# Rank counts on two engines, narrower rows and unread products in the selection of a gated recurrence with a capacity-limited mixture of experts

## The chip, the cores and the metric

The kernel runs on one core of a Trainium2 chip. A core has five engines with queues of their own: TensorE (PE, matmuls; PEld is its weight load), VectorE (DVE), ScalarE (ACT), GpSimd (POOL) and SyncE (SP, which here issues the large transfers), beside 16 DMA engines. The metric is the device time of one execution in microseconds, 254.26 as the median of three runs before the change (253.77 to 255.12).

## The reference, cut to what matters

```python
sig = 1.0 / (1.0 + np.exp(-f_logit))                 # x, f_logit: (4, 5056, 256)
f = lower_bound + (1.0 - lower_bound) * sig
for t in range(S):
    h = f[:, t] * h + (1.0 - f[:, t]) * x[:, t];  y[:, t] = h
X = y.reshape(20224, 256);  logits = X @ w_gate      # 8 experts
expert_idx = argmax(logits);  gate_w = softmax(logits)[expert_idx]
for e in range(8):                                   # the 80 tokens of highest gate_w among e's
    tok = top_80(gate_w[expert_idx == e])
    out[tok] = gate_w[tok, None] * (np.maximum(X[tok] @ w1[e], 0.0) @ w2[e])   # F = 1024
# every other row of out is zero
```

## The kernel before, in words

Stage 1 (to about 145 us). Forty units of 512 tokens of one sequence (the last group 448) are loaded, turned to channels on PE (`sp`, `up`, L226), scanned on DVE (L243), kept in SBUF as `h_all`, and multiplied with the gate weights (`lg`, L255). For each group of four units the logits are turned (`lt`, L270), the largest is taken and the softmax value of the chosen expert is turned back (`ct`, L343) into `cand`: 128 rows, one for each expert and each position modulo 16, with 1280 candidates each. SP's queue carries loads, and among them writes of zeros that clear the output (L149).

Stage 2, the selection. Each row's 16 highest values are found (`vals`, L496 to 499). The rows of an expert must agree on its 80 highest: `spread` and a matmul with `mates` put the 16 x 16 values of an expert's rows side by side in PSUM (`rivals`, 256 columns, L506). For each of a row's 16 values one DVE instruction counts how many rivals are greater (`beat`, `rank`, L524). `taken` marks ranks under 80; two matmuls sum the counts (`sums_p`, L533, L534); `put` makes one-hot slots (L544), and 16 matmuls place token numbers and values in `flat_p` (L547). From it come `trow` (token numbers as integers, L549), the slots turned to partitions (`slots_down`, L479 to 486) and `doubts`, flags for a slow branch that does the selection in full if a row has more than 16 candidates of use. `max_index` (L511) and POOL (L467 to 518) find the token numbers meanwhile.

Stage 3, the experts. `gather` copies the 80 columns of an expert from `h_all`, with three engines side by side: DVE 28, ACT 28, POOL 24 columns. `scaled` (DVE), `hidden` (first layer, `h_ps`, L612), `relu` (ACT, L620), `result` (second layer, `y_ps`, L627), `finish` (DVE) and `scatter` (POOL) follow. Each engine works its queue in the order in which the code records it: the order is written out by hand. Weights arrive in halves of 512 KB in a ring of 7 buffers, in the order of a list (`order`); three entries (6 halves) are issued before the last clears, the rest as buffers come free (`more`), each issue standing in SP's queue.

Of the kernel before, what the change touches and what calls it, by code (L numbers as in the profile page):

```python
# [23 lines left out]
def kernel(  # L24
# [23 lines left out]
    DEEP = 2 * TOP  # L48
# [82 lines left out]

    hpool = tc.alloc_tile_pool(name="hpool", bufs=1, side="right")
# [23 lines left out]
    def clear_rest():  # L156
        clear_some(len(zeros) % R)
        for k, _ in zeros[::R]:
            clear(k)
        zeros.clear()  # L160

    with tc.tile_pool(name="ld", bufs=4) as ld, \
# [119 lines left out]
        def shifted(g):  # L282
            by_token(g)
            n_p = run(g)
            lg, _ = lts[g]
            full = [n_p, C, E]
            if g == begin(g):
                shs[g] = gsm.tile([P, per_batch, C, E], F32, name="shift", tag="shift")
                ohs[g] = gsm.tile([P, per_batch, C, E], BF16, name="oh", tag="oh", bufs=2)
                if any(run(k) < P for k in range(*batch_of(g))):  # L290
                    nc.gpsimd.memset(shs[g], 0.0)
            mx = gsm.tile([P, C], F32, name="mx", tag="mx")[:n_p]
            nc.vector.tensor_reduce(mx, lg, AX.X, ALU.max)  # L293
            nc.vector.tensor_tensor(lg, lg, mx.unsqueeze(2).broadcast_to(full), ALU.subtract)  # L294
            nc.scalar.copy(shs[begin(g)][:n_p, g - begin(g)], lg)  # L295
# [138 lines left out]
    order = [(1, 0)]  # L434
    for e in range(E):
        order += ([(1, e + 1)] if e + 1 < E else []) + [(2, e)]
# [54 lines left out]
    with tc.tile_pool(name="sel", bufs=1) as sel, \  # L491
         tc.tile_pool(name="psl", bufs=1, space=PSUM) as psl:
        vals = sel.tile([P, DEEP], F32, name="vals")
        rest = sel.tile([P, NP * TOP], F32, name="rest")
        flat_tops = tops.rearrange("p n t -> p (n t)")
        nc.vector.max(out=vals[:, :TOP], in_=flat_tops)  # L496
        nc.vector.match_replace(out=rest, in_to_replace=vals[:, :TOP], in_values=flat_tops,
                                imm_value=-2.0)
        nc.vector.max(out=vals[:, TOP:], in_=rest)
# [5 lines left out]
        rivals = psl.tile([P, C * DEEP], F32, name="rivals", tag="rivals")  # L505
# [3 lines left out]
        at = sel.tile([P, DEEP], U32, name="at")  # L509
        for k in range(0, DEEP, TOP):  # L510
            nc.vector.max_index(out=at[:, ds(k, TOP)], in_max=vals[:, ds(k, TOP)],  # L511
                                in_values=cand)
        ids = sel.tile([P, DEEP], F32, name="ids")
# [7 lines left out]
        rank = sel.tile([P, DEEP], F32, name="rank")  # L521
        beat = sel.tile([P, C * DEEP], F32, name="beat")
# [3 lines left out]
        taken = sel.tile([P, DEEP], F32, name="taken")  # L526
        some = sel.tile([P, DEEP], F32, name="some")
        count = sel.tile([P, 1], F32, name="count")
        nc.vector.tensor_scalar(some, vals, 0.0, None, ALU.is_gt)
        nc.vector.scalar_tensor_tensor(out=taken, in0=rank, scalar=float(capacity), in1=some,  # L530
                                       op0=ALU.is_lt, op1=ALU.mult, accum_out=count)
        sums_p = psl.tile([P, 2], F32, name="sums_p", tag="sums_p")
        nc.tensor.matmul(sums_p[:, 0:1], before, count, start=True, stop=True)  # L533
        nc.tensor.matmul(sums_p[:, 1:2], mates, count, start=True, stop=True)  # L534
# [3 lines left out]
        off = sel.tile([P, 2], F32, name="off")  # L538
# [6 lines left out]
        flat_p = psl.tile([2 * E, K], F32, name="flat_p", tag="flat_p")  # L545
        for j in range(DEEP):
            nc.tensor.matmul(flat_p, what[:, DEEP - 1 - j].rearrange("p i e -> p (i e)"),  # L547
                             put[:, j], start=j == 0, stop=j == DEEP - 1)
        nc.vector.tensor_copy(trow, flat_p[:E])  # L549
        flat = consts.tile([2 * E, K], F32, name="flat")  # L550
        nc.vector.tensor_copy(flat, flat_p)

        low = sel.tile([P, DEEP], F32, name="low")
        d = doubts
        nc.gpsimd.tensor_scalar(out=low, in0=taken, scalar1=-2.0, scalar2=2.0,
                                op0=ALU.mult, op1=ALU.add)
        nc.gpsimd.tensor_tensor(low, low, vals, ALU.add)
# [7 lines left out]
        nc.vector.tensor_scalar(d[:, 3:4], off[:, 1:2], float(capacity), None, ALU.is_gt)  # L567
        slots_down(flat, psl)
# [6 lines left out]
    def experts(again):  # L575
        with tc.tile_pool(name="xp", bufs=2) as xp, \
             tc.tile_pool(name="mp", bufs=2) as mp, \
             tc.tile_pool(name="psd", bufs=1, space=PSUM) as psd, \
# [77 lines left out]
            for e in range(E):  # L656
# [11 lines left out]
                if e > 0:  # L668
                    scatter(e - 1)
# [92 lines left out]
```

## Time and profile before

| | |
|---|---|
| runs, us | 254.26, 255.12, 253.77 |
| the profiled execution | 254.13 us, of which its span is 252.2 |
| busy: PE, DVE, ACT, POOL | 198.6 (79%), 171.5 (68%), 134.3 (53%), 135.5 (54%) us |
| mean granted clock of TensorE | 0.899 |
| moved by DMA | 81.09 MB, mean 321 GB/s |

Busy time is an average over three stages with different limits, so the share of an engine says little here. The profile's slices show where the stages lie, the chain of waits shows which work ended last, and the timeline shows single instructions with the idle time of their engine before them. A matmul of f32 operands shows as two instructions.

### The profile page before, as it was taken

How to read it: one execution, taken by the hardware profiler on the slowest of the kernel's cores; microseconds unless marked ns; L12 is line 12 of the kernel's file. 1: busy time of each engine (PE TensorE's matmuls, PEld its weight loads, DVE VectorE, ACT ScalarE, POOL GpSimd, SP SyncE). 2: the span in 40 equal slices, each digit the busy share in tenths (PEclk: the TensorE clock that was granted, in tenths of full speed). 3: DMA queues.
4: the chain of work that ended last, by engine and by line, in shares of the span. 5: the costliest groups of instructions: out<-in, count | busy, mean ns of one | idle time of the engine just before them, and what ended most of it. 6: DMA issues, size and time to landing. Idle time of an engine off the chain costs nothing.

```text
span 252.2 us, 5978 instructions
## 1 busy us (share of the span) xinstructions
PE 198.6 (79%) x1755; PEld 155.6 (62%) x1755; DVE 171.5 (68%) x484; ACT 134.3 (53%) x390; POOL 135.5 (54%) x275
## 2 busy tenths in 40 slices
PE   0679999999998799999699832016199999999990
PEld 0567676767675577667466521016199788888860
DVE  0898879696967697898689677982655066656200
ACT  1678868686879677767958510000625545455100
POOL 2758769595865969675669110300764066661111
PEclk9999999999999999999999965557555899999997
DMA  6999999999999999999999999999954599999700
GB/s 176 382 386 384 384 382 394 390 390 391 395 386 391 392 390 392 393 391 389 318 313 360 304 380 408 347 321 318 295 184 148 187 276 312 318 305 306 241 18 21
DMA packets 59384, 81.09 MB, mean 321 GB/s; under 512 B 3280, under 2 KB 52048, under 8 KB 56912
## 3 DMA queue, kind: packets, MB, share of 16 engines
q1 hardware_dynamic: 57888, 78.92, 90.9%
q10 hardware_dynamic: 1072, 1.06, 1.2%
q0 software_dynamic: 384, 0.66, 0.8%
q8 instruction: 16, 0.26, 0.4%
q14 instruction: 24, 0.20, 0.3%
HBM read 78.91 MB, written 22.41 MB: 402 GB/s over the span
## 4 chain that ended last, share of the span: by engine, by line
PE 56%; DMA 10%; DVE 9%; issue 8%; ACT 7%; POOL 4%; SPq 3%; POOLq 0%; DVEq 0%; ACTq 0%
PE h_ps L612 14%; PE y_ps L627 11%; PE lg L255 10%; PE sp L226 9%; PE up L226 7%; DMA x_t<-in_x_dram 4%; POOL x_t L219 4%; ACT h_all L237 4%; DVE beat L524 3%; DMA out_dram<-z_dram 3%; DMA f_t<-in_f_logit_dram 3%; DVE h_all L243 2%; PE flat_p L547 2%; PE lt L270 2%; ACT ls L262 1%
## 5 line engine op out<-in xcount | busy, mean ns | idle before, releaser
L219 POOL TENSOR_TENSOR x_t<-f_t,x_t 128x1024 f32<-128x1024 f32 (+1 forms) x40 | 94.8, 2377 | 39.3 <-ACT f_t L215 22.0
L243 DVE TENSOR_TENSOR_SCAN h_all<-h_all,up 128x512 f32<-128x512 f32 (+1 forms) x80 | 95.2, 1240 | 5.2 <-ACT h_all L237 4.3
L237 ACT ACTIVATE h_all<-sp,nomlb 128x512 f32<-128x512 f32 (+1 forms) x80 | 50.1, 677 | 15.3 <-PE sp L226 15.1
L226 PE MATMUL sp<-ident,f_t 128*128 128x128 f32 (+1 forms) x320 | 45.0, 285 | 10.4 <-ACT f_t L215 8.2
L226 PEld LDWEIGHTS sp<-ident,f_t 128*128 128x128 f32 (+1 forms) x320 | 35.5, 145 | 26.9 <-issue 21.1
L255 PE MATMUL lg<-h_all,wg 128*32 128x128 f32 (+1 forms) x640 | 43.5, 401 | 5.2 <-ACT ls L262 3.7
L226 PE MATMUL up<-ident,x_t 128*128 128x128 f32 (+1 forms) x320 | 43.1, 277 | 4.7 <-POOL x_t L219 2.7
L215 ACT ACTIVATE f_t<-f_t 128x1024 f32<-128x1024 f32 (+1 forms) x40 | 42.6, 1064 | 6.9 <-DMA f_t<-in_f_logit_dram 6.7
L612 PE MATMUL h_ps<-xt,w_sb 128*128 128x80 f32 x256 | 36.4, 311 | 7.0 <-issue 7.0
L594 ACT COPY xe<-h_all 128x2 f32 x224 | 22.2, 191 | 36.5 <-issue 30.4
L612 PEld LDWEIGHTS h_ps<-xt,w_sb 128*128 128x128 f32 x256 | 36.1, 227 | 7.8 <-issue 7.3
L226 PEld LDWEIGHTS up<-ident,x_t 128*128 128x128 f32 (+1 forms) x320 | 36.2, 143 | 7.0 <-POOL x_t L219 4.1
L594 DVE COPY xe<-h_all 128x2 f32 x224 | 26.6, 180 | 14.7 <-issue 14.7
L594 POOL COPY xe<-h_all 128x2 f32 x192 | 24.2, 193 | 15.0 <-DVE goal L486 8.2
L627 PE MATMUL y_ps<-w_sb,hid 128*80 128x256 f32 x128 | 29.6, 387 | 0.0
L255 PEld LDWEIGHTS lg<-h_all,wg 128*32 128x32 f32 x640 | 18.1, 118 | 18.2 <-ACT ls L262 5.9
L636 POOL DMA_INDIRECT out_dram<-y,goal x8 | 7.5, 939 | 32.4 <-DVE y L633 30.0
L627 PEld LDWEIGHTS y_ps<-w_sb,hid 128*80 128x80 f32 x128 | 19.2, 154 | 7.9 <-issue 0.7
L620 ACT ACTIVATE hid<-h_ps 128x320 f32<-128x320 f32 x16 | 7.0, 436 | 22.5 <-PE h_ps L612 18.1
L633 DVE TENSOR_SCALAR y<-y_ps,gsl 80x256 f32<-80x256 f32 x8 | 3.8, 480 | 19.9 <-PE y_ps L627 19.9
L295 ACT COPY shift<-lt 128x128 f32<-128x128 f32 (+1 forms) x10 | 2.6, 265 | 16.6 <-DVE lt L294 16.6
L293 DVE TENSOR_REDUCE mx<-lt 128x16 f32<-128x128 f32 (+1 forms) x10 | 2.9, 291 | 12.5 <-PE lt L270 12.3
(103 smaller groups left out, 104.8 us busy)
## 6 DMA issues: line engine op xcount, KB each, us to landing
f_t<-in_f_logit_dram SPq DMA_DIRECT2D x36, 512.0 KB, 7.0
x_t<-in_x_dram SPq DMA_DIRECT2D x36, 512.0 KB, 7.4
w_sb<-in_moe_w_dram SPq DMA_DIRECT2D x32, 512.0 KB, 4.7
out_dram<-z_dram SPq DMA_DIRECT2D x40, 256.0 KB, 7.3
out_dram<-z_dram SPq DMA_DIRECT2D x9, 1024.0 KB, 17.4
f_t<-in_f_logit_dram SPq DMA_DIRECT2D x4, 448.0 KB, 7.5
x_t<-in_x_dram SPq DMA_DIRECT2D x4, 448.0 KB, 7.7
z_dram<-zero ACTq DMA_DIRECT2D x1, 1024.0 KB
```

Of the source, the lines that this page charges most:

```text
L215: nc.scalar.activation(s_t, s_t, ACT.Sigmoid, scale=-1.0)
L219: nc.gpsimd.tensor_tensor(u_t, sts[n], u_t, ALU.mult)
L226: nc.tensor.transpose(ps[:, ds(r * k, k)], src[n][:, r, ds(o * P, P)], ident[:k, :k])
L237: nc.scalar.activation(columns(n, o), sps.pop((n, o)), ACT.Identity, scale=nomlb[:, ds(o, 1)], bias=1.0)
L243: nc.vector.tensor_tensor_scan(h, h, ups.pop((n, o)), h_all[:, o, ds(spot(n) - 1, 1)] if n >= B else 0.0, ALU.mult, ALU.add)
L255: nc.tensor.matmul(lgs[g][ds(r * LC, LC), b, :k], wg[:, o], columns(n, o)[:, r::R], start=o == 0, stop=o == DC - 1, skip_group_check=True)
L524: nc.vector.tensor_scalar(beat, rivals, vals[:, ds(k, 1)], 0.0, ALU.is_gt, ALU.add, accum_out=rank[:, ds(k, 1)])
L594: copy(X[e][:, :, ds(k + j, 1)], h_all[:, :, ds(v, 1)])
L612: nc.tensor.matmul(h_ps[:, c], halves[i][:, o, ds(c * P, P)], xt[:, o], start=o == 0, stop=o == DC - 1, skip_group_check=True)
L620: nc.scalar.activation(HID[e][:, ds(i * CH, CH)], ps[i], ACT.Relu)
L627: nc.tensor.matmul(y_ps, hid[:, c], halves[c // CH][:, c % CH], start=c == 0, stop=c == FC - 1)
L636: nc.gpsimd.indirect_dma_start(out=out, out_offset=bass.IndirectOffsetOnAxis(ap=goal[:, ds(e, 1)], axis=0), in_=Y.pop(e), in_offset=None, ...
```

## The change

- **Depth.** A row keeps 12 values instead of 16 (`DEEP`), so `rivals` has 192 columns, `put` 960 and the placing 12 matmuls.
- **Ranks on two engines.** DVE counts for 5 of them (`BY_DVE`); ACT takes the other 7, each as a sum of signs over `rivals`, recorded ahead of DVE's. Two small instructions join the two.
- **Unread products.** `busy` records plain products of the identity on PE, whose results nobody reads: 14 ahead of the last `ct`, 8 behind it, 20 behind `rivals`, 4 behind `sums_p`, 22 behind the first gather.
- **Order.** The slots and the doubts move from the end of the selection into `settle`, called within expert 0 and done on DVE alone. Expert 0's second layer now stands ahead of expert 1's first; the weight list has (2, 0) ahead of (1, 1).
- **Columns.** DVE 24, ACT 32, POOL 24.
- **Pad.** A tile of 32 bytes that nobody uses stands ahead of the load buffers.

```diff
-    DEEP = 2 * TOP
+    DEEP = 3 * TOP // 2
+    BY_DVE = 5
...
+    consts.tile([P, 8], F32, name="pad")
...
+    def busy(pool, m, tag):
+        warm = pool.tile([P, P], F32, name="warm", tag=tag)
+        for _ in range(m):
+            nc.tensor.matmul(warm, ident, ident, start=True, stop=True)
...
         shifted(n_grp - 1)
+        busy(pss, 14, "sp")
         chosen(n_grp - 1)
         some_of(of_batch, -1)
+        busy(pss, 8, "sp")
...
-    order = [(1, 0)]
-    for e in range(E):
+    order = [(1, 0), (2, 0), (1, 1)]
+    for e in range(1, E):
...
+        busy(psl, 20, "kept")
...
+        for k in range(BY_DVE, DEEP):
+            nc.scalar.activation(signs, rivals, ACT.Sign, scale=-1.0, bias=vals[:, ds(k, 1)],
+                                 accum_out=rank2[:, ds(k, 1)])
...
-        for k in range(DEEP):
+        nc.vector.tensor_scalar(some, vals, 0.0, 0.0, ALU.is_gt, ALU.add, accum_out=count[:, 1:2])
+        for k in range(BY_DVE):
             nc.vector.tensor_scalar(beat, rivals, vals[:, ds(k, 1)], 0.0, ALU.is_gt, ALU.add,
                                     accum_out=rank[:, ds(k, 1)])
...
+        nc.vector.tensor_copy(rank2[:, :BY_DVE], rank)
+        nc.vector.tensor_scalar(rank2[:, BY_DVE:], rank2[:, BY_DVE:], -0.5, 0.5 * (M - 1),
+                                ALU.mult, ALU.add)
...
+        busy(psl, 4, "kept")
...
-        nc.vector.tensor_copy(flat, flat_p)
+        nc.scalar.copy(flat, flat_p)
+
+    def settle():
...
-    ways = [(mybir.EngineType.DVE, nc.vector.tensor_copy, 28),
-            (mybir.EngineType.Activation, nc.scalar.copy, 28),
+    ways = [(mybir.EngineType.DVE, nc.vector.tensor_copy, 24),
+            (mybir.EngineType.Activation, nc.scalar.copy, 32),
...
-            for e in range(2):
-                gather(e)
-                scaled(e)
+            gather(0)
+            scaled(0)
+            if not again:
+                busy(psl, 22, "rivals")
+            gather(1)
+            scaled(1)
             ps = hidden(0)
             relu(0, ps)
             more(1)
+            gather(2)
+            y_ps = result(0)
+            more(1)
+            scaled(2)
             if not again:
-                total = psd.tile([1, 4], F32, name="total")
+                settle()
+            finish(0, y_ps)
+            ps = hidden(1)
+            relu(1, ps)
+            more(1)
```

On PE, from the last turn of logits to the placing, there stood before:

```order
L270 MATMUL lt<-ident,ls 112x128 x4
L343 MATMUL ct<-ident,gm 128x112
L506 MATMUL rivals<-spread,mates 128x256
L533 MATMUL sums_p<-count,before 128x1
L534 MATMUL sums_p<-count,mates 128x1
L547 MATMUL flat_p<-put,what 16x80 x16
```

and on PE at the same place there stand now (`warm` is the unread product, `kept` holds what `flat_p` held, and the sums share the tile of `rivals`):

```order
L280 MATMUL lt<-ident,ls 112x128 x4
L170 MATMUL warm<-ident 128x128 x14
L353 MATMUL ct<-ident,gm 128x112
L170 MATMUL warm<-ident 128x128 x8
L521 MATMUL rivals<-spread,mates 128x192
L170 MATMUL warm<-ident 128x128 x20
L561 MATMUL rivals<-count,before 128x1
L562 MATMUL rivals<-count,mates 128x2
L170 MATMUL warm<-ident 128x128 x4
L577 MATMUL kept<-put,what 16x80 x12
```

Four groups of unread products stand in the queue, each ahead of a matmul that the selection waits for. On PE, from there into the experts, before:

```order
L481 MATMUL sp_t<-ident,flat 80x16
L612 MATMUL h_ps<-xt,w_sb 128x80 x16
L655 MATMUL total<-doubts,ones 1x4
L612 MATMUL h_ps<-xt,w_sb 128x80 x16
L627 MATMUL y_ps<-w_sb,hid 80x256 x8
```

and on PE now, behind the placing:

```order
L170 MATMUL warm<-ident 128x128 x22
L643 MATMUL h_ps<-xt,w_sb 128x80 x16
L658 MATMUL y_ps<-w_sb,hid 80x256 x8
L492 MATMUL kept<-ident,flat 80x16
L643 MATMUL h_ps<-xt,w_sb 128x80 x16
L699 MATMUL total<-doubts,ones 1x4
```

The turn of the slots went from ahead of the experts to behind expert 0's second layer, which moved ahead of expert 1's first. On DVE, in the ranks, with the engines that an instruction waits for, before:

```order
L463 TENSOR_SCALAR parts_i<-at 128x16 [waits DVE_49]
L465 TENSOR_SCALAR parts_i<-at 128x16
L524 TENSOR_SCALAR beat,rank<-rivals,vals 128x256 [waits PE_49]
L524 TENSOR_SCALAR beat,rank<-rivals,vals 128x256 [waits DVE_49] x15
L529 TENSOR_SCALAR some<-vals 128x16
L530 SCALAR_TENSOR_TENSOR taken,count<-rank,some 128x16 [waits DVE_49]
```

and on DVE now:

```order
L477 TENSOR_SCALAR parts_i<-at_2043 128x12
L551 TENSOR_SCALAR some,count<-vals_2002 128x12
L553 TENSOR_SCALAR beat,rank<-rivals,vals_2002 128x192 [waits PE_49,Activation_49]
L553 TENSOR_SCALAR beat,rank<-rivals,vals_2002 128x192 [waits DVE_49] x4
L555 COPY rank_2033<-rank 128x5 [waits DVE_49]
L556 TENSOR_SCALAR rank_2033<-rank_2033 128x7
L559 SCALAR_TENSOR_TENSOR taken,count<-rank_2033,some 128x12 [waits DVE_49]
```

Eleven compares left DVE, and its first one has a wait for ACT that it had not.

## Rows read from the trace of the kernel before

**Rows 1.** The page's 40 slices: TensorE's granted clock in tenths.

```profile
PEclk9999999999999999999999965557555899999997
```

**Rows 2.** The chain of waits from 168 us on: start us, length us, what.

```profile
core 0 of [0], span 252.2 us
...
182.11 7.09 PE h_ps L612 x32
...
189.32 7.04 PE h_ps L612 x32
196.37 4.27 PE y_ps L627 x16
200.63 3.53 PE h_ps L612 x32
204.16 3.46 PE y_ps L627 x16
...
239.11 6.92 PE y_ps L627 x32
```

**Rows 3.** Windows: length, engines' busy us, then PEclk, DMA share, GB/s.

```profile
146.50:147.00 0.50, 0.00 (x0) 0.00 (x0) 0.50 (x4) 0.43 (x1) 0.00 (x0) 0.68 1.09 389
173.50:174.00 0.50, 0.50 (x6) 0.50 (x5) 0.00 (x0) 0.00 (x0) 0.00 (x0) 0.51 1.19 360
197.50:198.00 0.50, 0.50 (x3) 0.33 (x2) 0.00 (x0) 0.00 (x0) 0.00 (x0) 0.62 0.73 131
184.00:186.00 2.00, 2.00 (x11) 2.00 (x11) 2.00 (x19) 0.00 (x0) 0.53 (x5) 0.50 0.33 123
```

**Rows 4.** Timeline of PE, 148 to 157: start, length, what, idle before.

```profile
149.05 1.06 PE L270 MATMUL lt<-ident,ls 128*112 128x128 f32 x4
153.50 0.42 PE L343 MATMUL ct<-ident,gm 112*128 112x112 f32 x1 [3.39 <-DVE gm L333]
156.39 1.19 PE L506 MATMUL rivals<-spread,mates 128*128 128x256 f32 x2 [2.47 <-DMA out_dram<-z_dram]
```

**Rows 5.** Timeline of DVE: first and last of 16 compares, and taken.

```profile
159.17 0.48 DVE L524 TENSOR_SCALAR_CACHE_REDUCE beat<-rivals,vals 128x256 f32<-128x256 f32 x1
...
167.08 0.48 DVE L524 TENSOR_SCALAR_CACHE_REDUCE beat<-rivals,vals 128x256 f32<-128x256 f32 x1
...
167.70 0.17 DVE L530 SCALAR_TENSOR_TENSOR taken<-rank,some 128x16 f32<-128x16 f32 x1
```

**Rows 6.** Groups by form on ACT: count | busy us, mean ns | idle before.

```profile
L237 ACT ACTIVATE h_all<-sp,nomlb 128x512 f32<-128x512 f32 x72 | 45.5, 682 | 12.8 <-PE sp L226 12.6
...
L620 ACT ACTIVATE hid<-h_ps 128x320 f32<-128x320 f32 x16 | 7.0, 436 | 22.5 <-PE h_ps L612 18.1 <-issue 4.1 <-ACT xe L594 0.3
...
L295 ACT COPY shift<-lt 128x128 f32<-128x128 f32 x9 | 2.4, 265 | 12.8 <-DVE lt L294 12.8
```

**Rows 7.** The chain of waits, count to placing: start us, length us, what.

```profile
167.93 0.59 PE sums_p L533 x2
...
169.18 0.90 DVE put L544
...
170.22 4.18 PE flat_p L547 x32
```

**Rows 8.** Timeline of the first gathers on ACT and DVE.

```profile
176.86 2.74 ACT L594 COPY xe<-h_all 128x2 f32 x28 [25.38 <-issue]
177.94 0.75 DVE L594 COPY xe<-h_all 128x2 f32 x6 [2.12 <-issue]
179.00 2.61 DVE L594 COPY xe<-h_all 128x2 f32 x22 [0.31 <-issue]
181.24 2.74 ACT L594 COPY xe<-h_all 128x2 f32 x28 [1.64 <-issue]
181.75 0.43 DVE L601 TENSOR_SCALAR xt<-xe,omlb 128x80 f32<-128x80 f32 x2
```

**Rows 9.** SP's issue of expert 2's first half of w1, and its landing.

```profile
L444 SPq DMA_DIRECT2D w_sb<-in_moe_w_dram x1: 374/374/374, 165.2 to 165.2; - x1
...
DMA to landing us min/median/max: 23.0/23.0/23.0
```

More of the change, by code (lines that the diff above doesn't have):

```diff
@@ L489 @@
     doubts = consts.tile([P, 6], F32, name="doubts")
[L491 to L493 removed]
+    psl = ctx.enter_context(tc.tile_pool(name="psl", bufs=1, space=PSUM))
+    with tc.tile_pool(name="sel", bufs=1) as sel:
+        vals2 = consts.tile([P, 2 * TOP], F32, name="vals2")
         rest = sel.tile([P, NP * TOP], F32, name="rest")
         flat_tops = tops.rearrange("p n t -> p (n t)")
[L496 to L497 removed]
+        nc.vector.max(out=vals2[:, :TOP], in_=flat_tops)
+        nc.vector.match_replace(out=rest, in_to_replace=vals2[:, :TOP], in_values=flat_tops,
                                 imm_value=-2.0)
[L499 removed]
+        nc.vector.max(out=vals2[:, TOP:], in_=rest)
+        vals = vals2[:, :DEEP]
         spread = sel.tile([P, C, DEEP], F32, name="spread")
@@ L504 @@
                                 place.unsqueeze(2).broadcast_to([P, C, DEEP]), ALU.mult)
-        rivals = psl.tile([P, C * DEEP], F32, name="rivals", tag="rivals")
+        M = C * DEEP
+        rivals = psl.tile([P, M + 3], F32, name="rivals", tag="rivals")
+        sums_p = rivals[:, M:]
+        rivals = rivals[:, :M]
         nc.tensor.matmul(rivals, mates, spread.rearrange("p c k -> p (c k)"),
                          start=True, stop=True)
-        at = sel.tile([P, DEEP], U32, name="at")
-        for k in range(0, DEEP, TOP):
-            nc.vector.max_index(out=at[:, ds(k, TOP)], in_max=vals[:, ds(k, TOP)],
+        busy(psl, 20, "kept")
+        rank = sel.tile([P, BY_DVE], F32, name="rank")
+        rank2 = sel.tile([P, DEEP], F32, name="rank2")
+        beat = sel.tile([P, M], F32, name="beat")
+        signs = sel.tile([P, M], F32, name="signs")
+        for k in range(BY_DVE, DEEP):
+            nc.scalar.activation(signs, rivals, ACT.Sign, scale=-1.0, bias=vals[:, ds(k, 1)],
+                                 accum_out=rank2[:, ds(k, 1)])
+        at2 = sel.tile([P, 2 * TOP], U32, name="at2")
+        for k in range(0, 2 * TOP, TOP):
+            nc.vector.max_index(out=at2[:, ds(k, TOP)], in_max=vals2[:, ds(k, TOP)],
                                 in_values=cand)
+        at = at2[:, :DEEP]
         ids = sel.tile([P, DEEP], F32, name="ids")
@@ L519 @@
                                     mine.unsqueeze(1).broadcast_to(share), ALU.mult)
-        rank = sel.tile([P, DEEP], F32, name="rank")
-        beat = sel.tile([P, C * DEEP], F32, name="beat")
-        for k in range(DEEP):
+        some = sel.tile([P, DEEP], F32, name="some")
+        count = sel.tile([P, 2], F32, name="count")
+        nc.vector.tensor_scalar(some, vals, 0.0, 0.0, ALU.is_gt, ALU.add, accum_out=count[:, 1:2])
+        for k in range(BY_DVE):
             nc.vector.tensor_scalar(beat, rivals, vals[:, ds(k, 1)], 0.0, ALU.is_gt, ALU.add,
                                     accum_out=rank[:, ds(k, 1)])
[L526 to L534, printed above, removed]
+        nc.vector.tensor_copy(rank2[:, :BY_DVE], rank)
+        nc.vector.tensor_scalar(rank2[:, BY_DVE:], rank2[:, BY_DVE:], -0.5, 0.5 * (M - 1),
+                                ALU.mult, ALU.add)
+        taken = consts.tile([P, DEEP], F32, name="taken")
+        nc.vector.scalar_tensor_tensor(out=taken, in0=rank2, scalar=float(capacity), in1=some,
+                                       op0=ALU.is_lt, op1=ALU.mult, accum_out=count[:, 0:1])
+        nc.tensor.matmul(sums_p[:, 0:1], before, count[:, 0:1], start=True, stop=True)
+        nc.tensor.matmul(sums_p[:, 1:3], mates, count, start=True, stop=True)
         nc.vector.tensor_tensor(what.rearrange("p k i e -> p k (i e)"),
@@ L537 @@
                                 taken.unsqueeze(2).broadcast_to([P, DEEP, 2 * E]), ALU.mult)
-        off = sel.tile([P, 2], F32, name="off")
+        busy(psl, 4, "kept")
+        off = consts.tile([P, 3], F32, name="off")
         nc.vector.tensor_copy(off, sums_p)
@@ L544 @@
         nc.vector.tensor_scalar(put, at_slot, off[:, 0:1], None, ALU.is_equal)
-        flat_p = psl.tile([2 * E, K], F32, name="flat_p", tag="flat_p")
+        kept = psl.tile([P, K + 2 * E], F32, name="kept", tag="kept")
+        flat_p = kept[:2 * E, :K]
         for j in range(DEEP):
@@ L548 @@
                              put[:, j], start=j == 0, stop=j == DEEP - 1)
+        flat = consts.tile([2 * E, K], F32, name="flat")
         nc.vector.tensor_copy(trow, flat_p[:E])
-        flat = consts.tile([2 * E, K], F32, name="flat")
-        nc.vector.tensor_copy(flat, flat_p)
-        low = sel.tile([P, DEEP], F32, name="low")
+        nc.scalar.copy(flat, flat_p)
+    def settle():
+        low = consts.tile([P, DEEP], F32, name="low")
         d = doubts
-        nc.gpsimd.tensor_scalar(out=low, in0=taken, scalar1=-2.0, scalar2=2.0,
+        slots_down(flat, kept[:K, ds(K, 2 * E)])
+        nc.vector.tensor_scalar(out=low, in0=taken, scalar1=-2.0, scalar2=2.0,
                                 op0=ALU.mult, op1=ALU.add)
-        nc.gpsimd.tensor_tensor(low, low, vals, ALU.add)
+        nc.vector.tensor_tensor(low, low, vals, ALU.add)
         nc.vector.tensor_reduce(d[:, 4:5], low, AX.X, ALU.min)
@@ L652, in experts @@
             more(1)
+            gather(2)
+            y_ps = result(0)
+            more(1)
+            scaled(2)
             if not again:
-                total = psd.tile([1, 4], F32, name="total")
+                settle()
[3 more added lines that the diff above has]
+            more(1)
+            if not again:
+                total = psl.tile([1, 4], F32, name="total", tag="rivals")
                 nc.tensor.matmul(total, ones, doubts[:, :4], start=True, stop=True)
-            for e in range(E):
+            for e in range(1, E):
                 if e + 2 < E:
@@ L667, in experts @@
                 finish(e, y_ps)
-                if e > 0:
-                    scatter(e - 1)
+                scatter(e - 1)
                 if e == 1 and not again:
```

8 lines of the change are left out of this document (3 added, 5 removed).

## The prediction

> **What bounds the kernel now.** I read the views in this order. The 40 slices show three stages: up to slice 23 of 40 (145 us) TensorE (PE) has the full granted clock; in slices 24 to 32 the clock is 5 to 8 tenths; then it is full again [rows 1]. The change acts from the second stage on. The chain of waits for that part runs through PE alone from 182.11 to 246.03: sixteen pieces, one expert's first layer (h_ps) and second layer (y_ps) in turn [rows 2]. A first layer takes 7.09 and 7.04 us in the first two pieces and 3.53 later, a second layer 4.27 in its first piece and 3.46 later (6.92 for the last two). The windows say why: the granted clock is 0.50 (1.2 GHz) there and returns to 1.0 (2.4 GHz) inside 197.5 to 198 [rows 3]. Before 182.11 lies a serial selection: turn, compare, count, place, gather [rows 4 to 8]. Last, the transfer queue: the first half of expert 2's first-layer weights is issued at 165.2, behind the clearing of the output, and lands 23.0 us later, at 188.2 [rows 9]. Nobody waits for it now, since PE wants it at 200.63. That number is what I build on.
>
> **The selection, part by part.** Times are those of the profiled execution: span 252.2, run 254.13, that is 1.93 around the span, and 0.05% under the median of 254.26.
>
> *The 14 products ahead of the last turn (ct).* One product is two matmul instructions of 128 columns, as each f32 product in the trace. An instruction costs 7.09/32 = 0.22 us at 0.50 and 3.53/32 = 0.11 at 1.0 by the h_ps pieces [rows 2], whose stationary tile is 128x128 too. So 14 take 6.2 us slow or 3.1 fast. They start when lt ends, 149.05 + 1.06 = 150.11, and ct is ready at 153.50 [rows 4]: 3.4 us of cover. The clock fell inside 146.5 to 147, so they begin slow. The one stream in the trace that brought it back with PE idle before is flat_p: it starts at 170.22 and the clock is up at the end of 173.5 to 174 [rows 3, 7]. The same 3.8 us here means 8 or 9 products slow and the rest fast. Bounds 0 and +2.8; I take the middle, **+1.4**.
>
> *The next 8 and 20.* Between ct's end (153.92) and rivals (156.39) lie 2.5 us [rows 4]; 8 fast products take 1.8. The 20 take 4.4 fast, from the end of rivals near 157 to 161.4, while the ranks need until 163. Nothing, as long as the clock is up; slow, they cost 1.0 and 2.7.
>
> *Ranks.* Sixteen compares start every (167.08 - 159.17)/15 = 0.53 us, and taken ends at 167.88 [rows 5]. Now 5 are left on VectorE (DVE), on 192 columns instead of 256: 0.53 less 64 columns at 0.48/256 each is 0.41; with the fixed part kept I take 0.46, so 2.3 us. Seven go to ScalarE (ACT). The order's rows show that they do not run beside each other: the first compare on DVE waits for ACT. A sign activation with an accumulated sum is not in the trace. The nearest rows are 265 ns (128x128 copy), 436 (128x320) and 682 (128x512 with a per-partition operand) [rows 6]; and each waits for the one before. I take 0.50, bounds 0.27 and 0.68. From rivals' end, 156.9 (its 1.19 us shrinks with columns and clock), seven end at 160.4; DVE is free at 159.2 plus `some`. Then 2.3 for the compares and 0.45 for the two small fix-ups and taken: 163.15 against 167.88, **-4.7** (bounds -5.7, where ACT is done before DVE is free, and -3.4).
>
> The Trainium skill, PSUM — Partial Sum Buffer, section "PSUM bank collisions raise a hardware error", says that two engines may not touch one bank's quadrant at the same time, reads included; the order obeys it. Without that wait the term would be -5.7.
>
> *Count, place.* sums_p to the end of put is 167.93 to 170.08 [rows 7]; put has 960 of 1280 columns (-0.2) and the two sums run at the fast clock (-0.2): **-0.4**. The 4 products (0.9) fit beside off and put. flat_p drops from 32 instructions to 24: 4.18 x 24/32 = 3.1 slow, 1.6 fast. **-2.6**, at worst -1.05.
>
> *Gather of expert 0.* From flat_p's end (174.40) to the first h_ps are 7.7 us. DVE ends it: it must first do the doubts and slots, starts copying at 177.94 and has 22 of its 28 copies from 179.00 on, 0.119 each; xt follows at 181.75 [rows 8]. After: the slots are moved behind, so DVE starts 1.15 earlier with 4 copies fewer (0.5). ACT does 32 at 2.74/28 = 0.098: from 176.86 to 180.0 on the old scale. Both then end near 180.0, **-1.6**. The 22 products (4.9 fast) lie inside the 6.1 us that remain.
>
> Sum: 182.11 + 1.4 - 4.7 - 0.4 - 2.6 - 1.6 = **174.2** for the first h_ps, bounds 171.8 and 178.5.
>
> **The experts.** Expert 0's first layer takes 3.53 at the full clock. Its second layer is now next and needs relu, which stands on ACT behind expert 1's gather: ACT ends gather 0 at 173.7, restarts 1.64 later [rows 8], copies 3.1, then relu 0.44: 179.0, 4.8 after the first h_ps. PE waits 1.3 there (new). Then 3.46, a transpose of 0.2, and expert 1's first layer 3.53: PE is free for expert 2 at 174.2 + 12.1 = 186.3. Where PE needed 18.5 us for these three pieces (182.11 to 200.63) it needs 12.1.
>
> Here the transfer takes over. The half for expert 2 is issued behind the clears, whose place in SP's queue the change does not touch; SP is not held by PE before it. So it still lands at 188.2, and PE **waits 1.9 us**. The halves behind it are issued earlier than before (as soon as experts 0 and 1 free their buffers) and then flow at one per 1.75 us of PE time, which the slices after 198 already carry. From expert 2's first layer on nothing else changes: 246.03 - 200.63 = 45.4. So 188.2 + 45.4 = 233.6, plus the tail of 6.2 to the span's end and 1.93: 241.7.
>
> **The clock in the gaps.** PE stands 1.2 us ahead of the first h_ps, 1.3 before relu, 1.9 before expert 2. In the trace the clock fell at 146.8 after pieces of lg with idle of about 1 us between them, and h_ps at 0.50 did not bring it back: it stayed low from 182.11 to 196.37 and rose only after some 1.5 us of y_ps [rows 2, 3]. So a fall in the last gap could cost expert 2's first layer 7.04 - 3.53 and its second 4.27 - 3.46: 4.3 together. Bounds 0 and 4.3; no row decides, since gaps of this kind beside h_ps do not occur. I take half, **+2.2**: 243.9.
>
> The Trainium skill, TensorE: Matmul & The Clock Gate, Part 1, says that the chip counts no instructions: sustained matmul activity releases the clock. Taken at its word for h_ps, expert 2's first layer would recover within itself after about flat_p's 3.8 us, and the loss would be 1.9 at most. The trace disagrees for h_ps (14 us at 0.50), so I keep 4.3 as the upper bound.
>
> **Parts at nothing.** The pad keeps the load buffers on the multiple of 256 bytes on which they stand now (the added constants and the pad together come to 256 bytes), and the loads' instructions are the same. The exchange of (2, 0) and (1, 1) in the load order touches transfers that land by 155, 20 us before use. The doubts on DVE (some 2 us) run while PE is in expert 0's second and expert 1's first layer; `total` on PE waits for them, about as long as it waits for the weights anyway.
>
> **Rivals.**
> 1. *The weights are no wait.* If expert 2's half lands before PE wants it, PE alone sets the end: 174.2 + 12.1 + 45.4 + 8.1 = 239.8. For it: only the last of the engines is late, the DMA share is 0.33 in 184 to 186 [rows 3]. Against: the landing is a row, and nothing ahead of it in the queue moves. 0.17.
> 2. *The clock is lost in full.* Every gap drops it, expert 2 runs at 0.50 through both layers: 241.7 + 4.3 = 246.0, or 247 with expert 0 slow too. For: h_ps never raised it. Against: y_ps of expert 0 streams right before. 0.20.
> 3. *The products hold PE up.* If the clock does not rise in the 14, all 68 run slow: ct ends at 156.8, the 8 at 160.3, the 20 at 170.0 (8.9 us), past the ranks, so sums at 171, flat_p from 172.8 to 175.9, the 22 to 185.6, and experts from 185.6 as before (63.9): 249.5 + 8.1 = 257.6, slower by 3.5. It decides against the change once the first h_ps comes after 182.1. Against: flat_p did raise the clock, and a 128-column product feeds PE as densely. 0.04.
> 4. *The change does not do what it says* (a row of the inputs needs more than 12 candidates, and the slow branch runs): counted from the inputs, the fullest of the 128 rows holds 9 of an expert's 80. 0.01.
>
> **How the numbers follow.** Forecast 0.58, with its own range 241 to 246; rivals as above. Eight in ten: from 240.0 (rival 1 half in) to 248.0 (rival 2 with a landing 1 us later). A change under about 0.5% (1.3 us) cannot be told from none here. Faster takes the forecast and rivals 1 and 2, less a little for a T near its late bound together with a slow clock: 0.94; same 0.02; slower 0.04.
>
> **What would show it.** In the profile after: ct near 155; the first compare on DVE starting when ACT's last sign ends, near 160; taken near 164.5; first h_ps near 174 lasting 3.5; y_ps next, 1.3 us of idle between; expert 2's first h_ps starting at a landing near 188; its length (3.5 or 7) tells the clock. A first h_ps after 178, or an h_ps of 7 in expert 0, would make the sum wrong; a start of expert 2 at 186 would be rival 1.

## The result and the profile after

The changed kernel takes 241.64 us as the median of four runs (241.20 to 242.21), the kernel before beside it 254.26. The ratio is 0.950, with a 95% interval of 0.947 to 0.954. The forecast was 243.9 with a range of 240 to 248. In only_22, columns_28_late and two_banks one execution in four came out 5.8 us or more above the others of its kernel; the medians and ratios given here leave it out.

The page's slices of the kernel after, TensorE's granted clock in tenths:

```profile
PEclk9999999999999999999999999799999999999997
```

Before, nine slices in a row (24 to 32) were under 9 [rows 1]; now one is, slice 26, beside the last one, which stands at 7 both times. Of the columns of windows, the last three are clock, DMA share and GB/s:

```profile
150.00:150.50 0.50, 0.50 (x5) 0.50 (x5) 0.50 (x3) 0.00 (x0) 0.00 (x0) 0.76 1.08 408
150.50:153.50 3.00, 3.00 (x16) 3.00 (x16) 2.08 (x8) 0.58 (x2) 0.25 (x1) 0.50 1.09 433
153.50:154.00 0.50, 0.50 (x5) 0.50 (x5) 0.03 (x1) 0.00 (x0) 0.00 (x0) 0.83 1.01 410
174.00:186.00 12.00, 10.40 (x75) 8.96 (x75) 7.97 (x65) 7.44 (x67) 8.48 (x67) 1.00 1.00 312
```

The clock falls near 150.3, when PE has been at work again for over a microsecond after the idle stretch ahead of the last `lt`, and is up again at 153.7, while the 14 products run. From there it is 1.00, and in 174 to 186 too, where the profile before has 0.50 [rows 3]. The timeline of PE (start, length, what, idle before):

```profile
149.28 0.60 PE L280 MATMUL lt<-ident,ls 128*112 128x128 f32 x4
149.72 4.92 PE L170 MATMUL warm<-ident 128*128 128x128 f32 x28
154.47 0.26 PE L353 MATMUL ct<-ident,gm 112*128 112x112 f32 x1
...
157.19 0.56 PE L521 MATMUL rivals<-spread,mates 128*128 128x192 f32 x2 [0.66 <-PE warm L170]
157.59 4.63 PE L170 MATMUL warm<-ident 128*128 128x128 f32 x40
164.42 0.38 PE L561 MATMUL rivals<-count,before 128*128 128x1 f32 x2 [2.20 <-DVE taken L559]
...
166.13 1.82 PE L577 MATMUL kept<-put,what 128*16 128x80 f32 x24
167.88 5.18 PE L170 MATMUL warm<-ident 128*128 128x128 f32 x44
174.22 3.77 PE L643 MATMUL h_ps<-xt,w_sb 128*128 128x80 f32 x32 [1.17 <-issue]
179.37 3.68 PE L658 MATMUL y_ps<-w_sb,hid 128*80 128x256 f32 x16 [1.38 <-ACT hid L651]
...
183.12 3.80 PE L643 MATMUL h_ps<-xt,w_sb 128*128 128x80 f32 x32
186.85 0.19 PE L699 MATMUL total<-doubts,ones 128*1 128x4 f32 x2
186.97 3.80 PE L643 MATMUL h_ps<-xt,w_sb 128*128 128x80 f32 x32
```

The first h_ps comes at 174.22 where it came at 182.11, and the pieces up to expert 2 take 12.75 us where they took 18.52 [rows 2]. The relu wait is there (1.38). Ahead of expert 2's first layer at 186.97 there is no idle time. ACT's first sign and DVE's first compare:

```profile
157.79 0.42 ACT L533 ACTIVATE signs<-rivals,vals 128x192 f32<-128x192 f32 x1 [6.12 <-PE rivals L521]
158.11 0.19 ACT L533 ACTIVATION_READ_ACCUMULATOR signs<-rivals,vals 128x1 f32 x1
158.33 0.42 ACT L533 ACTIVATE signs<-rivals,vals 128x192 f32<-128x192 f32 x1
...
161.60 0.42 DVE L553 TENSOR_SCALAR_CACHE_REDUCE beat<-rivals,vals 128x192 f32<-128x192 f32 x1 [1.44 <-ACT signs L533]
162.06 0.42 DVE L553 TENSOR_SCALAR_CACHE_REDUCE beat<-rivals,vals 128x192 f32<-128x192 f32 x1
...
164.18 0.17 DVE L559 SCALAR_TENSOR_TENSOR taken<-rank,some 128x12 f32<-128x12 f32 x1
```

Signs start 0.54 apart (0.42 and a read of the sum), compares 0.46; DVE stands 1.44 us until ACT's last sign. The sixteen compares before began at 159.17 and `taken` stood at 167.70 [rows 5]; now it is at 164.18. Last, SP's issue of expert 2's first weight half and its landing:

```profile
L456 SPq DMA_DIRECT2D w_sb<-in_moe_w_dram x1: 374/374/374, 163.8 to 163.8; - x1
...
who waited for it (us, times):
...
DMA to landing us min/median/max: 22.5/22.5/22.5
```

It lands at 163.75 + 22.5 = 186.2 (before 165.2 + 23.0 [rows 9]), 0.7 before PE wants it, and nobody waits.

### The profile page after: what moved, and what is told of

Same layout as the page of the kernel before. It is cut to its first block, busy times and chain, and to the rows that moved or that the text cites. A ratio compares the mean times of both kernels' runs of the same rounds, so it can differ in the third digit from the quotient of the medians.

```text
span 239.1 us, 6235 instructions
## 1 busy us (share of the span) xinstructions
PE 204.7 (86%) x1883; PEld 162.4 (68%) x1883; DVE 162.0 (68%) x434; ACT 140.2 (59%) x437; POOL 135.3 (57%) x273
## 3 DMA queue, kind: packets, MB, share of 16 engines
q10 hardware_dynamic: 1072, 1.06, 1.3%
## 4 chain that ended last, share of the span: by engine, by line
PE 38%; DMA 22%; issue 14%; ACT 9%; DVE 7%; POOL 5%; SPq 1%; POOLq 1%; DVEq 0%; ACTq 0%
PE lg L265 11%; DMA out_dram<-y,goal 10%; PE sp L236 10%; PE up L236 7%; PE warm L170 5%; DMA x_t<-in_x_dram 5%; DMA w_sb<-in_moe_w_dram 4%; ACT h_all L247 4%; DVE h_all L253 3%; DMA f_t<-in_f_logit_dram 3%; POOL x_t L229 3%; PE lt L280 2%; ACT ls L272 1%; ACT signs L533 1%; ACT f_t L225 1%
## 5 line engine op out<-in xcount | busy, mean ns | idle before, releaser
L625 ACT COPY xe<-h_all 128x2 f32 x256 | 25.4, 190 | 14.8 <-issue 8.9
L625 POOL COPY xe<-h_all 128x2 f32 x192 | 24.6, 200 | 14.3 <-issue 12.6
L625 DVE COPY xe<-h_all 128x2 f32 x192 | 22.7, 179 | 12.7 <-issue 12.7
L643 PEld LDWEIGHTS h_ps<-xt,w_sb 128*128 128x128 f32 x256 | 29.6, 192 | 1.9 <-issue 1.3
L643 PE MATMUL h_ps<-xt,w_sb 128*128 128x80 f32 x256 | 29.8, 275 | 1.2 <-issue 1.2
L658 PE MATMUL y_ps<-w_sb,hid 128*80 128x256 f32 x128 | 28.8, 380 | 1.4 <-ACT hid L651 1.4
L658 PEld LDWEIGHTS y_ps<-w_sb,hid 128*80 128x80 f32 x128 | 18.7, 150 | 9.0 <-ACT hid L651 1.5
L170 PE MATMUL warm<-ident 128*128 128x128 f32 x136 | 17.8, 294 | 0.0
L170 PEld LDWEIGHTS warm<-ident 128*128 128x128 f32 x136 | 17.3, 209 | 0.1
```

The lines of the kernel that those rows point to most:

```text
L170: nc.tensor.matmul(warm, ident, ident, start=True, stop=True)
L625: copy(X[e][:, :, ds(k + j, 1)], h_all[:, :, ds(v, 1)])
L643: nc.tensor.matmul(h_ps[:, c], halves[i][:, o, ds(c * P, P)], xt[:, o], start=o == 0, stop=o == DC - 1, skip_group_check=True)
L658: nc.tensor.matmul(y_ps, hid[:, c], halves[c // CH][:, c % CH], start=c == 0, stop=c == FC - 1)
```

## Experiments

The theory after the result: the end is set by PE from the last `ct` on. The selection moves the first h_ps; the products keep the clock up, in the placing and in expert 0's first layer above all; the parts at nothing (pad, load order, doubts) cost nothing. Rivals: the products only fill idle time and the gain is the ranks' and the order's; or one of the parts at nothing carries something.

**1. no_products.** All five groups out:

```diff
-        busy(pss, 14, "sp")
...
-        busy(pss, 8, "sp")
...
-        busy(psl, 20, "kept")
...
-        busy(psl, 4, "kept")
...
-                busy(psl, 22, "rivals")
```

> The changed kernel without any of the 68 unread products. Theory (the products earn the full clock in the first layers): the last turn 0.9 us earlier, placing and sums slow (+1.3 and +0.4), first h_ps near 175 at 0.50 and 7.0 long, y_ps of expert 0 partly slow (+0.8), the relu wait of 1.4 hidden: end 3.5 to 5 later, 245 to 247 us against 241.6. Rival (the gain came from ranks, depth, order and columns alone): 240.5 to 242. Rival (two first layers slow as in the kernel before): 248 to 249.

Measured: 245.45, ratio 0.965 (0.961 to 0.970). So the products are worth 3.8 of the 12.6 us. PE's timeline:

```profile
166.00 3.36 PE L573 MATMUL kept<-put,what 128*16 128x80 f32 x24 [1.10 <-DVE put L569]
175.63 7.08 PE L639 MATMUL h_ps<-xt,w_sb 128*128 128x80 f32 x32 [6.28 <-issue]
182.51 4.27 PE L654 MATMUL y_ps<-w_sb,hid 128*80 128x256 f32 x16
190.70 3.80 PE L639 MATMUL h_ps<-xt,w_sb 128*128 128x80 f32 x32
```

The first h_ps is 1.4 later (placing slow, 3.36), takes 3.3 longer, its y_ps 0.6 longer. The relu wait hides in the slow layer, and expert 2 is reached 3.7 later.

**2. no_last_22** (only the last line of that diff) and **3. only_22** (the four others).

> The changed kernel without the last group of 22. Theory: the clock falls in the 6.3 us between placing and first h_ps; expert 0's first layer takes 7.0, its end covers the relu wait, y_ps brings the clock back: 2.5 to 4.5 us later, 244 to 246. Rival (the 46 products ahead keep the clock over the gap): no change, 241.6.

> The changed kernel with the last 22 alone; the 46 ahead of the placing are gone. Theory: the last turn starts 0.9 earlier, rivals, sums and placing run slow (+0.3, +0.4, +1.3), the 22 bring the clock back before the first h_ps: about +1, 242 to 243. Rival (the 46 are what lifts the clock in time, the 22 alone are too few): first h_ps slow, 245 or more. Rival (the 46 only delay the turn): 241 or less.

Measured: without the 22, 244.93, ratio 0.964 (0.958 to 0.969); with them alone, 243.30, ratio 0.958 (0.952 to 0.964). Both are in the profile: without them h_ps starts on time and slow; with them alone it starts late and fast.

```profile
173.97 7.08 PE L643 MATMUL h_ps<-xt,w_sb 128*128 128x80 f32 x32 [6.28 <-issue]
```

```profile
175.90 3.77 PE L639 MATMUL h_ps<-xt,w_sb 128*128 128x80 f32 x32
```

The 22 are worth 3.3 us and the other 46 1.7. Together that is more than the 3.8 of all. In the profiles the difference lies in expert 0's y_ps, which takes 5.30 without the 22 and 4.27 without any product; why it is longer there is not shown.

**4. ranks_on_dve.** ACT's signs out, all twelve compares on DVE:

```diff
-    BY_DVE = 5
+    BY_DVE = 12
```

> The changed kernel with all 12 compares on DVE, none on ACT. The first compare can start at 160.2 instead of 161.6, then 12 x 0.46 = 5.5: taken at 166.0 against 164.4. Theory (PE's chain sets the end, each us ahead of the first h_ps counts in full): +1.7, 243.3. Rival (expert 2's weights set the end, some slack ahead of them): +1 or less. Rival (the wait between the engines ate the gain of ACT): no change.

Measured: 244.10, ratio 0.959 (0.955 to 0.965), 2.5 above the changed kernel where 1.7 was expected.

```profile
166.30 0.38 PE L559 MATMUL rivals<-count,before 128*128 128x1 f32 x2 [3.84 <-DVE taken L557]
168.08 3.26 PE L575 MATMUL kept<-put,what 128*16 128x80 f32 x24
```

From `ct` the sums come 1.64 later (166.30 - 154.71 against 164.42 - 154.47), which is the 1.7. The rest follows from it: the idle time behind the 20 products is 3.84 instead of 2.20, and the placing then runs slow, 3.26 instead of 1.82.

**5. no_pad.**

```diff
-    consts.tile([P, 8], F32, name="pad")
```

> The changed kernel without the 32-byte pad, so that the load buffers start at a multiple of 32 bytes but not of 64 or 256. Theory (alignment plays no part in this kernel's loads): no change, 241.6 within 0.5. Rival (loads into such buffers are slower): stage 1 longer, landing of the loads above 7.0 and 7.5 us, several us later.

Measured: 251.86, ratio 0.988 (0.985 to 0.992): 10 us worse, a clear miss. The page's loads, KB each and us to landing, of the kernel without the pad and of the changed kernel:

```profile
f_t<-in_f_logit_dram SPq DMA_DIRECT2D x36, 512.0 KB, 8.1
x_t<-in_x_dram SPq DMA_DIRECT2D x36, 512.0 KB, 9.1
```

```profile
f_t<-in_f_logit_dram SPq DMA_DIRECT2D x36, 512.0 KB, 7.0
x_t<-in_x_dram SPq DMA_DIRECT2D x36, 512.0 KB, 7.5
```

And where the last `lt` stands without it:

```profile
158.39 1.06 PE L279 MATMUL lt<-ident,ls 128*112 128x128 f32 x4
```

It comes at 158.39 instead of 149.28; what follows has the lengths of the changed kernel (h_ps 3.77 at 184.06). By the sizes of the tiles in the code (no view shows the addresses), the load buffers start at a multiple of 32 bytes only without the pad, and with it at a multiple of 256, as before the change. By the page's slices the loads move some 364 GB/s instead of 388 through all of stage 1, while the work on the loaded tiles keeps its length (ACT's `f_t` 1.06 us, POOL's `x_t` 2.38). The prediction was right to price the pad at nothing, since it keeps the alignment; left out, the added constants would have cost four fifths of the gain. This is one shift of the buffers: that it acts through the alignment is an inference, and which alignment would do was not tried.

**6. columns_28** (28, 28, 24 columns as before) and **7. old_expert_order** (expert 1's first layer ahead of expert 0's second, the weight list as before):

```diff
-    ways = [(mybir.EngineType.DVE, nc.vector.tensor_copy, 24),
-            (mybir.EngineType.Activation, nc.scalar.copy, 32),
+    ways = [(mybir.EngineType.DVE, nc.vector.tensor_copy, 28),
+            (mybir.EngineType.Activation, nc.scalar.copy, 28),
```

```diff
-    order = [(1, 0), (2, 0), (1, 1)]
+    order = [(1, 0), (1, 1), (2, 0)]
...
             more(1)
+            ps = hidden(1)
+            relu(1, ps)
+            more(1)
             gather(2)
             y_ps = result(0)
...
-            ps = hidden(1)
-            relu(1, ps)
-            more(1)
```

> The changed kernel with 28, 28, 24 columns. DVE's first gather ends 0.5 later and ACT's 0.4 earlier: first h_ps +0.2; relu of expert 0 waits for two gathers on ACT, 0.8 earlier in all, but the first h_ps is later. Theory: within 0.5 of 241.6. Rival (the split was worth something by itself): +1 or more.

> The changed kernel with expert 1's first layer ahead of expert 0's second again, and the weight list as before. Expert 1's first layer waits for its columns until 179.5 where expert 0's second now waits for relu until 179.4: theory: the order is worth nothing by itself, 241.6 within 0.7. Rival (the order hides the late weights or keeps the clock up): +1.5 to +4.

Measured: 247.69, ratio 0.971 (0.969 to 0.974), and 247.04, ratio 0.971 (0.966 to 0.976). Both missed, by 6 and 5 us. With 28 columns on DVE, PE's timeline and a window (clock third from last):

```profile
188.87 0.19 PE L699 MATMUL total<-doubts,ones 128*1 128x4 f32 x2 [1.97 <-DVE doubts L599]
189.00 7.11 PE L643 MATMUL h_ps<-xt,w_sb 128*128 128x80 f32 x32
```

```profile
189.00:192.00 3.00, 3.00 (x16) 3.00 (x15) 1.76 (x16) 2.73 (x28) 0.00 (x0) 0.50 1.06 392
```

With the old order:

```profile
164.25 0.38 PE L561 MATMUL rivals<-count,before 128*128 128x1 f32 x2 [2.19 <-DVE taken L559]
...
165.96 3.35 PE L577 MATMUL kept<-put,what 128*16 128x80 f32 x24
...
180.76 5.27 PE L643 MATMUL h_ps<-xt,w_sb 128*128 128x80 f32 x32 [1.40 <-DVE xt L632]
185.82 5.51 PE L658 MATMUL y_ps<-w_sb,hid 128*80 128x256 f32 x16
193.23 0.19 PE L699 MATMUL total<-doubts,ones 128*1 128x4 f32 x2 [1.76 <-DVE doubts L599]
193.35 3.79 PE L643 MATMUL h_ps<-xt,w_sb 128*128 128x80 f32 x32
```

The tiny matmul `total`, whose result nobody needs soon, stands in PE's queue ahead of expert 2's first layer and waits there for DVE's doubts. With 28 columns PE stands 1.97 us behind it, the clock falls, and the layer takes 7.11 instead of 3.80. With the old order expert 2 starts 6.4 us later than in the changed kernel (193.35 against 186.97): 1.8 is the wait for the doubts, after which the layer is fast (3.79), 3.2 is the low clock in expert 1's first and expert 0's second layer, and 1.4 is a placing that ran slow (3.35 instead of 1.82) ahead of everything that the order touches. So this run does not give the price of the order alone. In the changed kernel DVE has the doubts 0.7 us before `total` could start:

```profile
185.99 0.20 DVE L599 TENSOR_SCALAR doubts<-off 128x1 f32<-128x1 f32 x1
```

New theory: the columns matter through `total` alone. Rival: four more copies per gather on DVE make the gathers late.

**8. before_with_products.** The kernel before with the five groups of products at the same places, and nothing else of the change:

```diff
+        busy(pss, 14, "sp")
...
+        busy(pss, 8, "sp")
...
+        busy(psl, 20, "flat_p")
...
+        busy(psl, 4, "flat_p")
...
-            for e in range(2):
-                gather(e)
-                scaled(e)
+            gather(0)
+            scaled(0)
+            if not again:
+                busy(psd, 22, "total")
+            gather(1)
+            scaled(1)
```

> The kernel before with the five groups of products at the same places and nothing else of the change. Theory (the clock is the larger part): both first layers of 7.0 become 3.5, the first y_ps 0.8 shorter, placing about 2.1 shorter, the turn 0.9 later; then expert 2's weights and the wait for expert 1's columns take back 1 to 3: 246 to 249 against 254.3. Rival (ranks and depth are the larger part): 251 or more.

Measured: 250.81, ratio 0.984 (0.978 to 0.990), between the theory's range and the rival's. Its four runs lie in two pairs, 249.11 and 249.52 against 252.11 and 252.35; the profile is of the first:

```profile
182.79 3.80 PE L621 MATMUL h_ps<-xt,w_sb 128*128 128x80 f32 x32 [0.97 <-DVE xt L610]
188.28 3.80 PE L621 MATMUL h_ps<-xt,w_sb 128*128 128x80 f32 x32 [1.56 <-DVE xt L610]
195.37 3.69 PE L621 MATMUL h_ps<-xt,w_sb 128*128 128x80 f32 x32
```

The selection gains nothing (182.79 against 182.11): with sixteen compares PE idles 6.45 us behind the 20 products and the placing is slow, 3.43. The first layers run fast, but the second waits for DVE's gather (1.56). Expert 2 starts at 195.37 instead of 200.63 [rows 2]. That is 5.3 us in the profile and 4.0 by medians, near the 3.8 that the products are worth in the changed kernel; the pairs lie too far apart to say it closer.

**9. columns_28_late** is columns_28 with `total` recorded behind expert 1's second layer; **10. total_late** is the changed kernel with that move alone:

```diff
-            if not again:
-                total = psl.tile([1, 4], F32, name="total", tag="rivals")
-                nc.tensor.matmul(total, ones, doubts[:, :4], start=True, stop=True)
...
+                if e == 1 and not again:
+                    total = psl.tile([1, 4], F32, name="total", tag="rivals")
+                    nc.tensor.matmul(total, ones, doubts[:, :4], start=True, stop=True)
```

> Columns 28, 28, 24 again, with the one matmul total recorded behind expert 1's second layer instead of ahead of expert 2's first. Theory (columns_28 lost its 6 us because total stood in PE's queue and waited for DVE's doubts, and the clock fell behind that wait): expert 2's first layer follows expert 1's at about 187 and takes 3.8 us; total 241.5 to 243. Rival (the columns themselves cost it: DVE's copies make the gathers late): stays at 246.5 to 248.

> The changed kernel with total recorded behind expert 1's second layer. Theory (total waits for the doubts only a little or not at all with 24, 32, 24 columns, and expert 2's weights land at 186.2 to 186.6): 241.0 to 241.7, no difference of 0.5%. Rival (total's wait is part of why runs of the changed kernel differ by 1 us): 240.5 to 241 and all runs within 0.3 us.

Measured: 242.03, ratio 0.949 (0.941 to 0.956), and 242.00, ratio 0.950 (0.944 to 0.955). With 28 columns and `total` out of the way:

```profile
187.24 3.77 PE L643 MATMUL h_ps<-xt,w_sb 128*128 128x80 f32 x32 [0.45 <-DVE gsl L493]
```

The theory held: 5.7 of the 6 us are `total`'s place, and the split of the columns is worth nothing of its own that can be told. In the changed kernel the move gains nothing, since `total` does not wait there. What differs between the two profiles is the 14 products: in total_late's the clock fell two us earlier, they took 5.34 instead of 4.92, and `ct` came at 155.51 instead of 154.47.

**11. two_banks.** A second copy of `rivals` in a PSUM bank of its own, read by DVE:

```diff
+        rivals2 = psx.tile([P, M], F32, name="rivals2", tag="rivals2")
+        nc.tensor.matmul(rivals2, mates, spread.rearrange("p c k -> p (c k)"),
+                         start=True, stop=True)
...
-            nc.vector.tensor_scalar(beat, rivals, vals[:, ds(k, 1)], 0.0, ALU.is_gt, ALU.add,
+            nc.vector.tensor_scalar(beat, rivals2, vals[:, ds(k, 1)], 0.0, ALU.is_gt, ALU.add,
```

> The changed kernel with rivals computed a second time on PE into a PSUM bank of its own, which DVE's five compares read, so that they do not wait for ACT's signs. Theory (the prediction's -5.7 without the bank wait): the compares start near 159.5 to 160.2 instead of 161.6, the placing and the first h_ps come 1.4 earlier (172.8), and the end gains until expert 2's weights bind at 186.2 to 186.6: 240.6 to 241.2. Rival (ACT's signs are the longer of the two anyway, since taken needs both): taken 0.3 or less earlier, 241.3 to 242.

Measured: 241.27, ratio 0.947 (0.940 to 0.954): no gain that can be told. The first compare and PE's wait:

```profile
160.40 0.41 DVE L558 TENSOR_SCALAR_CACHE_REDUCE beat<-rivals,vals 128x192 f32<-128x192 f32 x1
...
163.15 0.17 DVE L564 SCALAR_TENSOR_TENSOR taken<-rank,some 128x12 f32<-128x12 f32 x1
```

```profile
187.60 3.77 PE L648 MATMUL h_ps<-xt,w_sb 128*128 128x80 f32 x32 [1.52 <-DMA w_sb<-in_moe_w_dram]
```

The compares run beside the signs, and `taken` comes 1.3 earlier counted from `ct`; the first h_ps comes at 173.26. PE is free for expert 2 at 186.1 and then waits 1.52 for the weights, issued at 164.67 and landing 22.8 later. This is the forecast's wait, in a kernel whose selection is a little quicker.

**12. combination.** Second bank, `total` late, and besides:

```diff
-    BY_DVE = 5
+    BY_DVE = 4
...
-        busy(pss, 14, "sp")
+        busy(pss, 9, "sp")
...
+    early[order[3] + (0,)] = half(*order[3], 0)
```

The last line issues expert 2's first weight half ahead of the last clears; its second half follows as a buffer comes free.

> Together: the second bank, four compares on DVE and eight signs on ACT, 9 products instead of 14 ahead of ct, the first half of expert 2's weights issued ahead of the last clears, total behind expert 1's second layer. Theory (the selection sets the time until the weights bind): ct 0.8 earlier, ranks 1.3 earlier, first h_ps near 172, expert 2 at 185 to 186; 239.3 to 240.7. Rival 1 (weights bind all the way, since the second half lands no earlier): 241 to 241.7. Rival 2 (9 products do not bring the clock back): 243 or more.

Measured: 240.29 (239.60 to 240.51), ratio 0.944 (0.938 to 0.949). All four of its runs are under all four of the changed kernel, and under all four of total_late, which was run beside it (241.55 to 242.12), so it is the quickest version here, by 0.6%. Which of its five parts gives how much was not taken apart.

```profile
172.41 3.77 PE L652 MATMUL h_ps<-xt,w_sb 128*128 128x80 f32 x32 [1.18 <-issue]
181.31 5.58 PE L652 MATMUL h_ps<-xt,w_sb 128*128 128x80 f32 x48
187.31 1.98 PE L652 MATMUL h_ps<-xt,w_sb 128*128 128x80 f32 x16 [0.41 <-DMA w_sb<-in_moe_w_dram]
```

Nine products bring the clock back in this run, and `ct` comes at 154.12. Expert 2's first half (the last 16 of the x48) runs on; now the second half of the weights is 0.41 late, and of the 1.8 us that the selection gained 1.4 arrive.

## Why the prediction was right, and where it was not

The profiled execution against the prediction's steps, in us:

| step | predicted | measured |
|---|---|---|
| `ct` later by the 14 products | +1.4 | +1.0 (154.47, was 153.50) |
| ranks, `ct` to `taken` | -4.7 | -4.5 |
| count and place up to `put` | -0.4 | -0.6 |
| placing | -2.6 | -2.4 (1.82, was 4.18) |
| gather of expert 0 | -1.6 | -1.4 |
| first h_ps at | 174.2 | 174.22 |
| from there to PE free for expert 2 | 12.1 | 12.75 |
| PE waits for expert 2's weights | 1.9 | 0 |
| expert 2 to the last y_ps | 45.4 | 45.65 |
| tail, and what lies around the span | 8.1 | 8.6 |
| clock in the gaps | +2.2 | 0 |

The time lies in the forecast's range, but two terms of the sum, the wait of 1.9 and the clock's 2.2, did not occur. What happened is rival 1, to which the prediction gave 0.17: PE alone sets the end. Of these 4.1 us 1.4 came back as small overruns in PE's pieces and the tail. Without them the profiled run would have taken rival 1's 239.8, under the range's lower end of 240.0, so it is in part luck that the number fell inside.

**The selection** came out term by term. Each term had a row for the same engine doing nearly the same. The first came out by another course, though: the prediction had the 14 products begin at the low clock, but they began at 1.00 and the clock fell under them at 150.3. Where it fell ahead of them, in total_late, `ct` came 2.0 later than before the change (155.51), still under the bound of 2.8. The one unseen operation, the sign with a sum, was taken as 0.50 and starts every 0.54. That the first compare waits for ACT was read from the order and is in the trace (1.44); two_banks prices it at 1.3, close to the 1.0 between the prediction's value and its lower bound. The Trainium skill, PSUM — Partial Sum Buffer, "PSUM bank collisions raise a hardware error", says that two engines may not access the same quadrant of one bank at the same time. The runs do not test it: in one bank the program's own wait puts the compares behind the last sign, in two they overlap the signs, and a collision no run shows.

**The clock in the gaps** is the step that failed: +2.2 was charged and nothing was lost. The 1.17 and 1.38 us of idle time left the clock at 1.00, and the third gap, which was to be the one that costs, was not there. The mechanism is real, as columns_28 shows: 1.97 us of waiting at the same place, and expert 2's first layer took 7.11 as the forecast's upper case has it, its second 5.26 instead of 3.62. The length of the gap alone does not sort the cases: 1.40 us went with a slow layer in old_expert_order, 1.52, 1.56 and 1.76 with fast ones in two_banks, before_with_products and old_expert_order. Even one and the same gap went both ways: PE idles 2.20 us ahead of the sums in the changed kernel and 2.19 in old_expert_order, with the same work around it, and the placing behind it took 1.82 in the first and 3.35 in the second. So a gap cannot be priced from its length alone, and what decides stays open.

The prediction held on rows that h_ps does not bring the clock back. It repeats: at the low clock h_ps takes 7.08 in no_products and 7.11 in columns_28, and the clock rises in the y_ps behind it. The Trainium skill, TensorE: Matmul & The Clock Gate, Part 1, says that sustained matmul activity releases the clock; for these layers the measurement decides against taking that at its word, while the unread products and y_ps do as it says.

**The weight wait** of 1.9 is the other step that failed, on the landing and not on the idea. The prediction said that nothing ahead of the half in SP's queue moves. The issue did come earlier, 163.75 instead of 165.2 [rows 9], and the landing was quicker by 0.5; PE came 0.65 later than thought. So the half was there 0.7 us ahead of its use and the time went as in rival 1, where PE alone sets the end. That rival's sum of 239.8 lacks the 0.65 in PE's pieces, 0.25 behind and 0.5 in the tail: 241.2, the profiled run. It is a near tie: two_banks, with PE 0.9 earlier and the issue 0.9 later, waits 1.52. In the changed kernel and those of its variants that keep the pad and issue the half behind the clears, the issue came at 162.7 to 164.7; what moves it was not traced.

**The parts at nothing.** The pad was right at nothing as long as it is there; the prediction knew the multiple of 256 but had no price for losing it, and no_pad gives 10 us. `total` was called harmless because PE would be waiting for weights anyway. It was harmless, for another reason: the doubts were done 0.7 us before. With the old column split the same matmul costs 5.7 us. With the old order the loss is 5.4, of which the wait for the doubts is only a part. So the split and the order, which the sum did not price by themselves, each went with nearly half of what the change gains; for the split the cause is shown, for the order it is not.

**The other rivals.** The products did not hold PE up beyond the 1.0 us at `ct`: 14 end at 154.6, the 20 at 162.2 with the sums at 164.42. The loss of the clock in full is what columns_28 shows. What the 12 values instead of 16 are worth by themselves no run shows.

## What to carry to other kernels

Where a chain of short waits lets TensorE's clock fall ahead of a layer that does not raise it, unread products in the idle stretches can be worth their queue space (3.8 us here), if they end about when the work behind them is ready. Look through the matmuls in PE's queue for those that nobody needs soon: one that waits for a busy engine stops the whole queue, and the clock can go with it. When constants are added ahead of large load buffers, keep the buffers where they were (here a pad of 32 bytes decided over 10 us), and price a part at nothing only together with the margin by which it costs nothing.

## What the runs showed of the hardware

- Loads of 512 KB land in 8.1 and 9.1 us instead of 7.0 and 7.5 when their buffers are moved by the 32 bytes of the pad, off a multiple of 256 by the sizes of the tiles.
- A sign activation over 128x192 with an accumulated sum takes 0.42 us and a read of the sum of 0.19; with each waiting for the one before they start every 0.54.
- An unread product of 128 columns takes 4.63/40 = 0.116 us per instruction at 1.0, with the clock held there.
- Nine such products brought the clock back in one profiled run: in combination it was up by 153.0; with 14 it was up at 153.7 in the changed kernel and at 154.6 in total_late.
- After idle gaps of 2.20 and 2.19 us in the same place TensorE's clock once stayed at 1.00 and once fell (the placing behind took 1.82 and 3.35).
